# Attention in its fixed order: reciprocal roots of the RMS norm on VectorE instead of ScalarE

## The chip, the cores and the metric

The kernel runs on one core of a Trainium2 chip. The metric is the device time of one execution in microseconds (us), as the median of several runs. Five engines take part: TensorE (PE: matmuls and transposes; PEld: its weight loads), VectorE (DVE), ScalarE (ACT), GpSimd (POOL) and SyncE (SP, which issues most DMAs). Each engine runs its own instructions in order and waits for the others by semaphores.

## The reference, cut to what matters

Three layers follow each other: an attention with RMS-normalised queries and keys, a dense layer pair, and a mixture of experts. The change lies in the norm of the attention.

```python
# q, k, v: (4, 12, 448, 64); g_q, g_k: (64,)
def rmsnorm(x, g):
    rms = np.sqrt(np.mean(x * x, axis=-1, keepdims=True) + 1e-06)
    return x / rms * g
q_n, k_n = (rmsnorm(q, g_q), rmsnorm(k, g_k))
scores = (1 / np.sqrt(64)) * np.matmul(q_n, k_n.transpose(0, 1, 3, 2))
scores = scores - np.max(scores, axis=-1, keepdims=True)
attn = np.exp(scores)
attn = attn / (np.sum(attn, axis=-1, keepdims=True) + 1e-09)
x = np.matmul(attn, v)                     # then (1792, 768)
h = x @ w_in; x = np.maximum(0.01 * h, h) @ w_out
# then: each row of x goes to the expert of its largest gate logit (8 experts)
```

## The kernel before

The attention works on pairs of heads: 4 batches with 6 pairs each make 24 pairs. For one pair, q and k lie in SBUF as 112 partitions by 4 rows of 64 numbers, for two heads; that is one tile `qk` of 112x1024. The steps of a pair are:

- `square`: ACT squares `qk` into `sq`, DVE sums each 64 numbers into `ms` (112x16 for a pair).
- `roots`: from `ms` the factors `y` = 1/sqrt(mean square + 1e-6). Mostly two pairs are taken together (112x32), in four of the 14 calls one pair (112x16). ACT computes Ln (`ln`), then Exp with scale -0.5 (a first `y`), its square (`a`) and -0.5 times the mean square (`hm`); DVE makes one Newton step of them with two instructions (lines 219 and 220).
- `norm`: POOL multiplies q or k by `y` (tile `qn`, line 238), 112x512 each; for the very first pair k is multiplied on DVE.
- `turn_q`, `turn_k`: PE transposes, ACT and DVE split the result into a high and a low part (`qh`, `ql`, `kh`, `kl`). The product g_q times g_k (`gg`) goes into the key side.
- `top`: PE multiplies queries by keys into the PSUM tile `tp`, of which there is one, and DVE takes the row maxima (`md`, line 275), four chunks per pair. `row` transposes the maxima into `mx`.
- `probs`: PE makes scores in the PSUM tile `sc`, of which there is one too, and ACT takes the Exp of them (`p`, or `pr` for the first of the four chunks; line 298).
- `values`, `sums`, `back`, `spread`, `scale`, `store`: PE multiplies by v (`av`, line 307), POOL adds the four `p` into `pr` (line 311), and the row sums divide the result.

A unit here is the work between one `pr` and the next: the scores and values of one pair, the row maxima of the next, and preparation of later ones. The first three units run by `begin`, the others by `steady`. Their order on PE, DVE, ACT and POOL is written out by hand (`tc.manual_schedule`). Two calls of `roots` come ahead of unit 0, two in unit 0, one each in units 2 and 3; then every second unit (5, 7, 9 and so on to 19) holds one, between the second and the third row maximum. From unit 8 on the units between them hold, at the same place, `work`: a decode of half a weight tile for the dense layers, five DVE instructions (lines 579 to 584), an ACT and a POOL instruction (line 586).

```python
            if begun and odd and three:
                self.norm(three, (1,))
            if begun and odd and self.group:
                self.roots(self.group)
                self.norm(four, (1,))
            self.work(i)
```

`three` and `four` are the pairs three and four ahead. After the attention the dense layers follow (`FirstMoe`, lines 614 to 669), then the routing and the experts; their order is set by a scheduler.

Of the kernel before, what the change touches and what calls it, by code (L numbers as in the profile page):

```python
# [9 lines left out]
F32 = mybir.dt.float32  # L10
F32R = mybir.dt.float32r
I32 = mybir.dt.int32
U32 = mybir.dt.uint32
AF = mybir.ActivationFunctionType
ALU = mybir.AluOpType
# [5 lines left out]
def attention_moe_moe2(  # L21
# [15 lines left out]
    nc = tc.nc  # L37
    P = 128
    B, H, S, DH = q.shape
# [6 lines left out]
    CP = 112  # L46
# [49 lines left out]
    nc.gpsimd.iota(pcol_i, pattern=[[0, 1]], base=0, channel_multiplier=1)  # L96
    pcol = cst.tile([P, 1], F32, name="pcol")
    nc.vector.tensor_copy(pcol, pcol_i)
    gg = cst.tile([P, 1], F32, name="gg")
    gk = cst.tile([P, 1], F32, name="gk")  # L100
    WG = 32
# [3 lines left out]
    def load_constants():  # L105
        for half in range(2):
            nc.scalar.dma_start(gg[half * DH:(half + 1) * DH, :], g_q.rearrange("(d o) -> d o", o=1))
            nc.scalar.dma_start(gk[half * DH:(half + 1) * DH, :], g_k.rearrange("(d o) -> d o", o=1))
        nc.vector.tensor_tensor(gg, gg, gk, ALU.mult)

    def load_gates():
        nc.sync.dma_start(wg[:, :, :NE], w_gate.rearrange("(c p) e -> p c e", p=P))
# [40 lines left out]
    class Attention:  # L153


        def __init__(self, pool, early, ps, pst):
            self.pool, self.early, self.ps, self.pst = pool, early, ps, pst
            self.PR, self.MX = [], []
            self.first = self.work = None
            self.after = []  # L160
            self.mask = pool.tile([P, CP], F32R, name="mask", bufs=1)
            self.eps = pool.tile([CP, 1], F32, name="eps", bufs=1)
            nc.vector.memset(self.eps, 1e-6)
            self.eps2 = pool.tile([CP, 1], F32, name="eps2", bufs=1)
            nc.vector.memset(self.eps2, -0.5e-6)
            nc.scalar.activation(self.mask, mrow.to_broadcast([P, CP]), AF.Copy)
            for i in range(2):
                pr = pool.tile([P, 2, S], F32, name=f"pr{i}", bufs=1)
                nc.vector.memset(pr, 1e-9)
                self.PR.append(pr)  # L170
            for i in range(2):
                md = pool.tile([CP, NC, P], F32, name=f"md{i}", bufs=1)
                nc.vector.memset(md, 0.0)
                self.MX.append(md)
# [13 lines left out]
        def square(self, st):  # L188

            n = 4 * NC  # L190
            flat = st["qk"].rearrange("p t h (c d) -> p (t h c) d", d=DH)
            sq = self.early.tile([CP, n, DH], F32, name="sq", bufs=2)
            for h in (slice(0, n // 2), slice(n // 2, n)) if st is self.first else (slice(0, n),):
                nc.scalar.activation(sq[:, h], flat[:, h], AF.Square)
                nc.vector.tensor_reduce(st["ms"][:, h], sq[:, h], AX.X, ALU.add)

        def together(self, sts):
# [7 lines left out]
        def roots(self, sts):  # L205

            ms = sts[0]["all"]
            n = 4 * NC
            w, full = n * len(sts), n * 2
            ln, hm, a, y0, y1 = (  # L210
                self.pool.tile([CP, full], F32, name=name, bufs=bufs)[:, :w]
                for name, bufs in (("ln", 1), ("hm", 1), ("a", 1), ("y0", 1), ("y", 3)))
            for i, st in enumerate(sts):
                st["yf"] = y1[:, i * n:(i + 1) * n]
            nc.scalar.activation(ln, ms, AF.Ln, scale=1.0 / DH, bias=self.eps)
            nc.scalar.activation(y0, ln, AF.Exp, scale=-0.5)
            nc.scalar.activation(a, y0, AF.Square)
            nc.scalar.activation(hm, ms, AF.Identity, scale=-0.5 / DH, bias=self.eps2)
            nc.vector.tensor_tensor(a, a, hm, ALU.mult)
            nc.vector.scalar_tensor_tensor(y1, a, 1.5, y0, ALU.add, ALU.mult)  # L220

        def tr(self):
            return self.ps.tile([P, S], F32, name="tr", bufs=TRB)
# [572 lines left out]
    att.first = att.load(0, 0)  # L796
    att.load_v(att.first)
    load_constants()
    wts = Weights()
    moe = FirstMoe(wts)  # L800
# [28 lines left out]
    y = my.tile([P, B, KD, S], F32, name="ysum")  # L829
# [280 lines left out]
```

## Time and profile before

| | |
|---|---|
| median of 3 runs | 1290.72 us (1290.34 to 1291.54) |
| profiled execution | 1289.88 us, of which its span is 1288.2 us |
| PE busy | 1179.9 us (92%) |
| DVE busy | 743.8 us (58%) |
| ACT busy | 544.9 us (42%) |
| POOL busy | 529.3 us (41%) |
| first `pr` | 24.87 us from the start |
| start of unit 21, the last but two | 339.24 us |

The times of a trace are counted from the start of its span. The busy shares are means over stages with different limits: the attention lies in about the first 400 us, the dense layers and the experts in the rest. An idle time in brackets stands before the instruction that ended it, with the engine that released it.

### The profile page before, as it was taken

The numbers are of one execution on the slowest core, as the hardware profiler recorded it, in microseconds if no ns is written. First come the engines' busy times: TensorE is split into PE (matmuls) and PEld (weight loads), VectorE is DVE, ScalarE is ACT, GpSimd is POOL, SyncE is SP. The second block draws the span as 40 slices with busy tenths as digits, with TensorE's granted clock in tenths as the row PEclk, the third lists the DMA queues.
The fourth block names the chain that finished last, engine by engine and source line by source line (L and its number), as shares of the span: only waits on it lengthen the run. The fifth ranks groups of instructions, "written<-read, shape, count | busy, mean of one in ns | idle before, by whom it ended". The sixth has DMA issues, their size and how long they took to land.

```text
span 1288.2 us, 19076 instructions
## 1 busy us (share of the span) xinstructions
PE 1179.9 (92%) x6988; PEld 943.5 (73%) x6988; DVE 743.8 (58%) x1166; ACT 544.9 (42%) x875; POOL 529.3 (41%) x365
## 2 busy tenths in 40 slices
PE   4779998998999988999999999999799999999997
PEld 2445554554556877888888888988678988898986
DVE  5555666665652788475857584235766149414556
ACT  5676667665533542222222222122435148324444
POOL 1555665665633554243434343120224126412334
PEclk9898989888989999999999999999979999999999
DMA  5211122101010222021212120052375229612456
GB/s 142 58 37 50 51 64 75 56 27 28 28 44 25 75 74 74 21 66 37 62 38 68 33 72 13 1 208 51 86 267 188 76 86 361 232 46 80 179 215 216
DMA packets 68082, 116.29 MB, mean 90 GB/s; under 512 B 6780, under 2 KB 45948, under 8 KB 67968
## 3 DMA queue, kind: packets, MB, share of 16 engines
q1 hardware_dynamic: 64528, 103.87, 25.4%
q0 software_dynamic: 3120, 11.02, 2.5%
q8 instruction: 57, 0.93, 0.3%
q14 instruction: 57, 0.47, 0.1%
q10 hardware_dynamic: 320, 0.00, 0.0%
HBM read 106.61 MB, written 12.58 MB: 93 GB/s over the span
## 4 chain that ended last, share of the span: by engine, by line
PE 65%; DVE 14%; ACT 7%; issue 6%; POOL 5%; DMA 2%; ACTq 0%; DVEq 0%; POOLq 0%; SPq 0%
PE sc L296 6%; PE av L307 6%; PE mp L644 4%; PE mo L625 4%; PE mo L626 4%; PE mo L627 4%; PE mp L645 4%; PE mp L646 4%; PE ph L988 3%; PE ph L986 3%; PE ph L987 3%; PE py L1004 3%; PE py L1002 3%; PE py L1003 3%; DVE top L581 2%
## 5 line engine op out<-in xcount | busy, mean ns | idle before, releaser
L311 POOL TENSOR_TENSOR pr<-pr,p 112x896 f32<-112x896 f32 x72 | 152.5, 2118 | 58.1 <-ACT p L298 35.5
L652 DVE TENSOR_TENSOR ysum<-mp,ysum 128x448 f32<-128x448 f32 x168 | 103.8, 621 | 113.0 <-PE mp L646 112.2
L644 PE MATMUL mp<-gh,w1h 128*128 128x448 f32 x384 | 145.6, 380 | 20.1 <-DVE ysum L652 16.4
L625 PE MATMUL mo<-xTh,w0h 128*128 128x448 f32 x384 | 142.2, 370 | 7.0 <-DVE g L632 3.4
L645 PE MATMUL mp<-gl,w1h 128*128 128x448 f32 x384 | 142.4, 371 | 0.0
L626 PE MATMUL mo<-xTl,w0h 128*128 128x448 f32 x384 | 142.0, 370 | 0.2 <-DVE xTl L63 0.2
L627 PE MATMUL mo<-xTh,w0l 128*128 128x448 f32 x384 | 141.2, 368 | 0.0
L646 PE MATMUL mp<-gh,w1l 128*128 128x448 f32 x384 | 140.8, 370 | 0.0
L63 POOL TENSOR_TENSOR gl<-g,gh 128x448 fp32r<-128x448 f32 x64 | 76.9, 1201 | 140.1 <-ACT gh L633 113.3
L586 POOL TENSOR_TENSOR raw<-raw,top 128x384 f32<-128x384 f32 x64 | 64.8, 1013 | 139.7 <-DVE raw L584 114.9
L275 DVE TENSOR_REDUCE md<-tp 112x2 f32<-112x896 f32 x96 | 104.5, 1089 | 23.6 <-PE tp L273 23.0
L1002 PE MATMUL py<-w2h,hT 128*128 128x384 f32 x288 | 99.7, 346 | 0.0
L644 PEld LDWEIGHTS mp<-gh,w1h 128*128 128x128 f32 x384 | 72.8, 190 | 35.3 <-DVE ysum L652 13.8
L1004 PE MATMUL py<-w2l,hT 128*128 128x384 f32 x288 | 96.8, 336 | 0.0
L1003 PE MATMUL py<-w2h,hL 128*128 128x384 f32 x288 | 96.5, 335 | 0.0
L988 PE MATMUL ph<-w1l,xgh 128*128 128x512 f32 x216 | 86.5, 400 | 4.2 <-DVE w1l L63 4.2
L986 PE MATMUL ph<-w1h,xgh 128*128 128x512 f32 x216 | 86.8, 402 | 0.0
L63 DVE TENSOR_TENSOR hL<-pt,hT 128x512 fp32r<-128x512 f32 x36 | 24.8, 689 | 106.2 <-ACTq L1012 59.4
L578 ACT ACTIVATE mag<-wd 128x384 f32<-128x384 f32 x64 | 35.4, 553 | 118.9 <-DVE top L581 62.3
L987 PE MATMUL ph<-w1h,xgl 128*128 128x512 f32 x216 | 85.6, 396 | 0.0
L625 PEld LDWEIGHTS mo<-xTh,w0h 128*128 128x128 f32 x384 | 72.4, 189 | 16.0 <-DVE g L632 3.7
L298 ACT ACTIVATE p<-sc 112x896 f32<-112x896 f32 x72 | 65.8, 913 | 42.0 <-PE sc L296 37.7
(200 smaller groups left out, 2583.0 us busy)
## 6 DMA issues: line engine op xcount, KB each, us to landing
r<-in_moe_w_dram SPq DMA_DIRECT2D x27, 1024.0 KB, 5.2
r<-in_moe_w_dram SPq DMA_DIRECT2D x36, 768.0 KB, 7.3
wd<-in_moe_w_in_dram SPq DMA_DIRECT2D x32, 384.0 KB, 3.3
wd<-in_moe_w_out_dram SPq DMA_DIRECT2D x32, 384.0 KB, 3.1
qk<-in_q_dram SPq DMA_DIRECT2D x24, 224.0 KB, 3.0
qk<-in_k_dram SPq DMA_DIRECT2D x24, 224.0 KB, 3.2
vv<-in_v_dram SPq DMA_DIRECT2D x24, 224.0 KB, 2.7
x2d<-xn SPq DMA_DIRECT2D x24, 224.0 KB, 2.9
```

The costliest lines, as they stand in the source:

```text
L311: nc.gpsimd.tensor_tensor(st["pr"][:CP], st["pr"][:CP], p, ALU.add)
L625: nc.tensor.matmul(ph, wh_[:, c], xh, start=(c == 0), stop=False)
L626: nc.tensor.matmul(ph, wh_[:, c], xl, start=False, stop=False)
L627: nc.tensor.matmul(ph, wl_[:, c], xh, start=False, stop=(c == KD - 1))
L644: nc.tensor.matmul(py, hi[:, sl], gh, start=(j == 0), stop=False)
L645: nc.tensor.matmul(py, hi[:, sl], gl, start=False, stop=False)
L646: nc.tensor.matmul(py, lo[:, sl], gh, start=False, stop=(j == GF - 1))
L986: nc.tensor.matmul(ph[n], xh[:, c], w1h[:, c, s_], start=(c == 0), stop=False)
L988: nc.tensor.matmul(ph[n], xh[:, c], w1l[:, c, s_], start=False, stop=(c == K1 - 1))
L1002: nc.tensor.matmul(py[n], hT[:, c], w2h[:, c, s_], start=(c == 0), stop=False)
L1003: nc.tensor.matmul(py[n], hL[:, c], w2h[:, c, s_], start=False, stop=False)
L1004: nc.tensor.matmul(py[n], hT[:, c], w2l[:, c, s_], start=False, stop=(c == K2 - 1))
```

## The change

The four ACT instructions of `roots` go, with their tables, and DVE does it all with nine small instructions: add 1e-6 to the sum, take the bits of the result as an integer times -0.5 plus a constant (a first estimate), then a cubic step of four instructions and a Newton step of three. The steps leave out constant factors; their product, `ROOT` squared for a query and a key, is divided out once in `gg`. The squares are scaled by 1/8 on ACT, so that their sum is the mean. Two constant tiles and their memsets go.

```diff
+    LAST = -21.33333396911621
+    ROOT = (LAST + 64 / 9) * 8 / 3
...
-        nc.vector.tensor_tensor(gg, gg, gk, ALU.mult)
+        nc.vector.scalar_tensor_tensor(gg, gg, ROOT ** -2, gk, ALU.mult, ALU.mult)
...
-            self.eps = pool.tile([CP, 1], F32, name="eps", bufs=1)
-            nc.vector.memset(self.eps, 1e-6)
-            self.eps2 = pool.tile([CP, 1], F32, name="eps2", bufs=1)
-            nc.vector.memset(self.eps2, -0.5e-6)
...
-                nc.scalar.activation(sq[:, h], flat[:, h], AF.Square)
+                nc.scalar.activation(sq[:, h], flat[:, h], AF.Square, scale=DH ** -0.5)
...
-            nc.scalar.activation(ln, ms, AF.Ln, scale=1.0 / DH, bias=self.eps)
-            nc.scalar.activation(y0, ln, AF.Exp, scale=-0.5)
-            nc.scalar.activation(a, y0, AF.Square)
-            nc.scalar.activation(hm, ms, AF.Identity, scale=-0.5 / DH, bias=self.eps2)
-            nc.vector.tensor_tensor(a, a, hm, ALU.mult)
-            nc.vector.scalar_tensor_tensor(y1, a, 1.5, y0, ALU.add, ALU.mult)
+            nc.vector.tensor_scalar(ms, ms, 1e-6, None, ALU.add)
+            nc.vector.tensor_scalar(
+                y.bitcast(I32), ms.bitcast(I32), -0.5, float(0x5F3759DF), ALU.mult, ALU.add)
+            nc.vector.tensor_tensor(a, y, y, ALU.mult)
+            nc.vector.tensor_tensor(a, a, ms, ALU.mult)
+            nc.vector.scalar_tensor_tensor(e, a, -10 / 3, a, ALU.add, ALU.mult)
+            nc.vector.scalar_tensor_tensor(y, e, 5.0, y, ALU.add, ALU.mult)
+            nc.vector.tensor_tensor(a, y, y, ALU.mult)
+            nc.vector.tensor_tensor(a, a, ms, ALU.mult)
+            nc.vector.scalar_tensor_tensor(y, a, LAST, y, ALU.add, ALU.mult)
```

On ACT, a steady unit with a root stood like this before, from the `pr` that starts the unit to the second `p` (`sp` holds row sums):

```order
L298 ACTIVATE pr_139<-sc 112x896
L254 ACTIVATE qh<-tr 128x448
L215 ACT_TABLE_LOAD
L215 ACTIVATE ln<-ms,eps 112x32
L216 ACT_TABLE_LOAD
L216 ACTIVATE y_1322<-ln 112x32
L217 ACTIVATE a<-y_1322 112x32
L218 ACTIVATE hm<-ms,eps_134 112x32
L298 ACTIVATE p<-sc 112x896
L323 COPY sp<-tr 128x224
```

The same stretch of ACT now (line numbers are two higher from `norm` on):

```order
L300 ACTIVATE pr_135<-sc 112x896
L256 ACTIVATE qh<-tr 128x448
L300 ACTIVATE p<-sc 112x896
L325 COPY sp<-tr 128x224
L300 ACTIVATE p<-sc 112x896
```

The six rows of lines 215 to 218 are gone between `qh` and `p`, and nothing has come in their place. Of 29 table loads one is left, ahead of the first ACT instruction.

On DVE, a steady unit with a root, from the low part of the keys to the reciprocal of the row sums (`r`), before:

```order
L266 SCALAR_TENSOR_TENSOR kl<-tr,gg,kh 128x448
L275 TENSOR_REDUCE md_141<-tp 112x2
L219 TENSOR_TENSOR a<-a,hm 112x32
L220 SCALAR_TENSOR_TENSOR y<-a,y_1619 112x32
L275 TENSOR_REDUCE md_141<-tp 112x2
L63 TENSOR_TENSOR ql<-tr,qh 128x448
L275 TENSOR_REDUCE md_141<-tp 112x2
L333 RECIPROCAL r<-av 112x8
```

The root's place on DVE now, from the row maximum ahead of it to `ql`:

```order
L277 TENSOR_REDUCE md_137<-tp 112x2
L213 TENSOR_SCALAR ms<-ms 112x32
L214 TENSOR_SCALAR y<-ms 112x32
L216 TENSOR_TENSOR a<-y 112x32
L217 TENSOR_TENSOR a<-a,ms 112x32
L218 SCALAR_TENSOR_TENSOR e<-a 112x32
L219 SCALAR_TENSOR_TENSOR y<-e,y 112x32
L220 TENSOR_TENSOR a<-y 112x32
L221 TENSOR_TENSOR a<-a,ms 112x32
L222 SCALAR_TENSOR_TENSOR y<-a,y 112x32
L277 TENSOR_REDUCE md_137<-tp 112x2
L63 TENSOR_TENSOR ql<-tr,qh 128x448
```

Nine rows stand where two stood; the root keeps its place among the row maxima. POOL's and SP's rows are the same in both kernels, in the same order. On PE two matmul groups of the dense layers (six instructions) stand eleven rows later than before; the rest is the same.

At the end of unit 0, the fourth root of the kernel stood on DVE before between the sums of squares and the halves of the next pair:

```order
L275 TENSOR_REDUCE md_143<-tp 112x2
L195 TENSOR_REDUCE ms<-sq 112x16
L219 TENSOR_TENSOR a<-a,hm 112x32
L220 SCALAR_TENSOR_TENSOR y<-a,y_375 112x32
L266 SCALAR_TENSOR_TENSOR kl<-tr,gg,kh 128x448
L63 TENSOR_TENSOR ql<-tr,qh 128x448
L275 TENSOR_REDUCE md_141<-tp 112x2 x2
```

And now:

```order
L193 TENSOR_REDUCE ms<-sq 112x16
L213 TENSOR_SCALAR ms<-ms 112x32
L214 TENSOR_SCALAR y<-ms 112x32
...
L222 SCALAR_TENSOR_TENSOR y<-a,y 112x32
L268 SCALAR_TENSOR_TENSOR kl<-tr,gg,kh 128x448
L63 TENSOR_TENSOR ql<-tr,qh 128x448
L277 TENSOR_REDUCE md_137<-tp 112x2 x2
```

Here too nine rows stand where two stood, ahead of `kl`, `ql` and the row maxima of unit 1.

## Rows read from the trace of the kernel before

**Rows 1.** The page's head: the span.

```profile
span 1288.2 us, 19076 instructions
```

**Rows 2.** The chain that ended last, 106 to 340 us, shares by engine and line.

```profile
by line: PE sc L296 25.5%; PE av L307 23.7%; PE tr L340 8.3%; PE tr L246 6.3%; PE tp L273 5.8%; ACT L215 4.4%; ACT L216 4.4%; PE av L330 3.9%; PE tr L280 3.6%; ACT p L298 2.8%; ACT qh L254 2.1%; PE tr L319 1.6%; DMA wd<-in_moe_w_out_dram 1.
```

**Rows 3.** Lines 215, 216, 219: ns min/median/max, first and last start; DVE's wait, times.

```profile
L215 ACT ACT_TABLE_LOAD  x14: 1283/1283/1283, 6.2 to 312.4; - x14
L215 ACT ACTIVATE ln<-ms,eps x14: 307/322/322, 8.8 to 313.7; 112x32 f32<-112x32 f32 x10, 112x16 f32<-112x16 f32 x4
...
L216 ACT ACT_TABLE_LOAD  x14: 1283/1283/1283, 9.1 to 314.0; - x14
...
L219 DVE TENSOR_TENSOR a<-a,hm x14: 166/192/1405, 11.1 to 316.0; 112x32 f32<-112x32 f32 x10, 112x16 f32<-112x16 f32 x4
...
  ACT hm L218: 49.8, 13
```

**Rows 4.** Windows of units: from:to, us; busy of PE, PEld, DVE, ACT, POOL; clock.

```profile
106.04:123.18 17.14, 14.70 (x106) 8.77 (x104) 8.38 (x13) 10.89 (x18) 9.26 (x7) 0.80 0.15 41
123.18:134.94 11.76, 11.76 (x106) 6.76 (x104) 7.95 (x11) 7.55 (x11) 7.30 (x5) 1.00 0.20 59
134.94:150.67 15.73, 13.29 (x106) 7.71 (x104) 8.35 (x13) 10.89 (x17) 9.29 (x7) 0.89 0.15 45
...
162.72:179.94 17.22, 14.78 (x106) 8.65 (x104) 8.34 (x13) 10.88 (x18) 9.78 (x7) 0.80 0.21 64
...
191.98:206.25 14.27, 11.83 (x106) 6.73 (x104) 8.25 (x13) 10.89 (x17) 9.39 (x7) 1.00 0.26 76
...
218.31:235.58 17.27, 14.83 (x106) 8.81 (x104) 8.38 (x13) 10.89 (x18) 9.58 (x7) 0.80 0.21 64
235.58:247.62 12.04, 12.03 (x106) 6.76 (x104) 10.20 (x16) 7.98 (x12) 7.91 (x6) 1.00 0.19 59
247.62:263.38 15.76, 13.32 (x106) 7.78 (x104) 8.35 (x13) 10.89 (x17) 9.59 (x7) 0.89 0.13 41
...
275.44:292.67 17.23, 14.79 (x106) 8.68 (x104) 8.35 (x13) 10.88 (x18) 9.77 (x7) 0.80 0.12 36
...
310.24:327.46 17.22, 14.84 (x106) 8.83 (x104) 7.13 (x12) 9.89 (x16) 9.24 (x7) 0.80 0.05 14
```

**Rows 5.** Timeline of unit 13, around its root: start us, us, engine, what.

```profile
220.50 1.28 ACT L215 ACT_TABLE_LOAD   x1
...
224.16 0.19 DVE L219 TENSOR_TENSOR a<-a,hm 112x32 f32<-112x32 f32 x1 [4.45 <-ACT hm L218]
224.39 0.19 DVE L220 SCALAR_TENSOR_TENSOR y<-a,y 112x32 f32<-112x32 f32 x1
...
224.98 0.65 PE L296 MATMUL sc<-qh,kh 64*112 64x448 f32 x2 [2.44 <-ACT p L298]
```

**Rows 6.** Timeline of unit 14, around its decode.

```profile
236.90 0.35 DVE L579 TENSOR_SCALAR top<-wd 128x384 int32<-128x384 int32 x1
...
239.68 1.09 DVE L275 TENSOR_REDUCE md<-tp 112x2 f32<-112x896 f32 x1
...
240.82 0.17 PEld L273 LDWEIGHTS tp<-kh,qh 64*112 64x112 f32 x2 [0.40 <-DVE md L275]
```

**Rows 7.** Timeline of unit 0, around the fourth root.

```profile
40.97 2.08 POOL L311 TENSOR_TENSOR pr<-pr,p 112x896 f32<-112x896 f32 x1
...
41.70 1.41 DVE L219 TENSOR_TENSOR a<-a,hm 112x32 f32<-112x32 f32 x1 [2.40 <-ACT hm L218]
...
42.15 1.01 PE L246 MATMUL tr<-ident,qn 112*128 112x112 f32 x4 [3.22 <-ACT mx L282]
```

**Rows 8.** Timeline around the second root, and of unit 2.

```profile
21.46 1.09 DVE L275 TENSOR_REDUCE md<-tp 112x2 f32<-112x896 f32 x1 [0.81 <-PE tp L273]
...
22.93 2.04 POOL L238 TENSOR_TENSOR qn<-qk,y 112x512 f32<-112x512 f32 x2 [9.85 <-DVE y L220]
...
68.93 0.19 DVE L219 TENSOR_TENSOR a<-a,hm 112x32 f32<-112x32 f32 x1 [3.72 <-ACT hm L218]
```

More of the change, by code (lines that the diff above doesn't have):

```diff
@@ L209, in roots @@
             w, full = n * len(sts), n * 2
-            ln, hm, a, y0, y1 = (
+            y, a, e = (
                 self.pool.tile([CP, full], F32, name=name, bufs=bufs)[:, :w]
-                for name, bufs in (("ln", 1), ("hm", 1), ("a", 1), ("y0", 1), ("y", 3)))
+                for name, bufs in (("y", 3), ("a", 1), ("e", 1)))
             for i, st in enumerate(sts):
-                st["yf"] = y1[:, i * n:(i + 1) * n]
-            nc.scalar.activation(ln, ms, AF.Ln, scale=1.0 / DH, bias=self.eps)
-            nc.scalar.activation(y0, ln, AF.Exp, scale=-0.5)
-            nc.scalar.activation(a, y0, AF.Square)
-            nc.scalar.activation(hm, ms, AF.Identity, scale=-0.5 / DH, bias=self.eps2)
-            nc.vector.tensor_tensor(a, a, hm, ALU.mult)
-            nc.vector.scalar_tensor_tensor(y1, a, 1.5, y0, ALU.add, ALU.mult)
+                st["yf"] = y[:, i * n:(i + 1) * n]
+            nc.vector.tensor_scalar(ms, ms, 1e-6, None, ALU.add)
[8 more added lines that the diff above has]
+            nc.vector.scalar_tensor_tensor(y, a, LAST, y, ALU.add, ALU.mult)
         def tr(self):
```

## The prediction

> **What bounds the kernel now.** I read the chain of waits first, for the stretch where the roots are computed. From 106 to 340 us PE's lines hold most of the chain, but ScalarE's lines 215 and 216 hold 4.4% each [rows 2]: 8.8% of 234 us, some 20 us, in which everything waited for ScalarE to change its table and take a logarithm and a first root. That is not what an average shows: ScalarE is busy only 42% of the span.
>
> Then the instructions of those lines. Each of the 14 roots loads a table twice, 1.283 us each time, and VectorE idles 49.8 us in 13 waits for the last of the four ScalarE instructions [rows 3], 3.83 us each.
>
> Third, one such wait in order of time [rows 5]. The table load begins at 220.50; VectorE's Newton step starts at 224.16 after 4.45 us of idling; PE gets its score tile back at 224.98 after 2.44 us of idling, because the Exp that empties the single score tile stands behind the root on ScalarE. So two chains cross the root: PE by way of that Exp, and VectorE's row maxima.
>
> Last, the units as windows [rows 4]. A unit with neither root nor decode takes 11.76 us and PE is busy in all of it; one with a decode 12.04. The eight units with a root take 17.14, 15.73, 17.22, 14.27, 17.27, 15.76, 17.23 and 17.22 us, together 131.84. Their PE clock column tells two costs apart. The unit of 14.27 us ran at full clock (1.00): its excess of 2.51 us over 11.76 is the stall of 2.44 us. The others show 0.80 or 0.89, so for part of the unit PE ran at 1.2 instead of 2.4 GHz, and PE's busy time grew from 11.83 to as much as 14.84 us. Each of these spells follows the stall, and the units without a stall have none.
>
> **The change, part by part.**
>
> *The eight steady roots.* All six rows of ScalarE go. What comes is nine small VectorE instructions, each needing the one before. The old pair of dependent ones started at 224.16 and 224.39 [rows 5], so 0.23 us apart, and I take 9 x 0.23 = 2.07 us for the new chain; the pair has the width of the new ones, and the operands of seven of them. Do they make PE wait in their turn? The decode answers it: at the same place in the unit VectorE is held from 236.90 to 239.68, 2.78 us, and PE then waits 0.40 us for the row maximum behind it [rows 6]. A block of 2.07 us is 0.71 us shorter, so PE should wait for nothing and the unit should become one without root: 11.76 us. Bounds: 11.76, as PE is then full, and 12.04, that of a unit with the longer block. The gain is 131.84 - 8 x 11.76 = 37.8 us, at the least 131.84 - 8 x 12.04 = 35.5. This contains the clock: 8 x 2.51 = 20.1 us of stall and 17.7 us of slow spells, which I expect to go with the stall that comes before each of them.
>
> POOL must not get in the way here. An old Newton step took 1.41 us instead of 0.19 when POOL was adding: it began at 41.70 and ended at 43.11, POOL's add ended at 43.05 [rows 7]. So VectorE's instructions on two SBUF tiles are held until POOL's running instruction ends. In a steady unit POOL's next product needs this very root and stands ahead of the adds, so POOL is idle meanwhile. The Trainium skill, in "SBUF — State Buffer", section "Who interferes with whom", says that a VectorE instruction with two SBUF inputs and a GpSimd instruction that reads SBUF exclude each other for the whole instruction. The trace agrees with its 1.41 us; the rule speaks against nine such instructions wherever POOL has work queued, and by it each of them could there wait for one add.
>
> *The roots ahead of the steady phase.* Here each goes by its own place, and bounds are wide. In general a root gives VectorE back its wait, 3.83 us on average [rows 3], and takes seven more instructions, 7 x 0.23 = 1.61: at best 2.2 us. Nothing is excluded down to zero where something else is late.
> - First root: from the logarithm's start at 8.8 to the Newton step at 11.1 and 0.4 us beyond, 2.7 us [rows 3]; now 2.1. Gain 0.6.
> - Second: the old ScalarE part was hidden behind the row maxima. The last of these ends at 22.55 and POOL takes the result at 22.93, 0.38 us later [rows 8]; now nine instructions stand behind that maximum. Loss 2.07 + 0.1 - 0.38, some 1.8 us.
> - Third: a wait of both chains, gain between 0 and 2.2; I take 1.2, as the later start takes half a microsecond and more of it.
> - Fourth: PE waited 3.22 us for ScalarE [rows 7], and that goes. But the adds are then queued on POOL and do not need this root, so the first new instruction waits for one add and lets the next add in ahead of the second instruction. VectorE then ends as late as before, and PE gains until it wants the row maxima behind it. Between 0 and 3.2; I take 1.0, nearer the blocked end, because of the 1.41 us.
> - Unit 2: VectorE's wait of 3.72 us [rows 8] less 1.61: 2.1. Unit 3: the same at best; I take 1.5.
>
> Sum 0.6 - 1.8 + 1.2 + 1.0 + 2.1 + 1.5 = 4.6 us; bounds from about -1 (only the second root's loss and half a microsecond of gain) to 9, and up to 3 us more for each slow spell that ends early there.
>
> *Costed at nothing.* The scale of the squares and the factor in `gg` change operands of instructions that are there anyway. The two memsets lie ahead of the first DMA's landing, with VectorE idle later; uncovered they would cost a tenth each. ScalarE's freed time beyond the waits (28 loads of 1.283 us and 56 small instructions) is worth nothing, since PE bounds the units. The six PE instructions that stand later in the dense layers I put at nothing, PE being busy before and behind them; a microsecond to either side if the order matters. SP's order is the same, and each load keeps its distance in units, which become 12 us instead of up to 17; they are 3 us transfers.
>
> **The sum.** 37.8 + 4.6 = 42.4 us off the profiled execution. That took 1289.88 us, 1.7 more than its span [rows 1], and lies 0.84 below the median of 1290.72. So 1289.88 - 42.4 = 1247.5; I say 1247.5 us, about 3.3% faster. What a measurement can tell from no change is 0.2%, 2.6 us.
>
> **The rivals.**
>
> *The fourth root is not blocked* (POOL lets the nine through, or they come between the adds). PE then keeps the 3.2 us instead of 1.0, and the slow spell of units 0 and 1 may shrink by up to 3: 1242. Against it the 1.41 us. Chance 0.14. With the forecast's 0.62 this makes the likeliest range 1240 to 1254.
>
> *Only the stalls go, and the slow spells stay*, because they come from the units' load and not from the idling. Then the eight units give 20.1 us and not 37.8: 1289.88 - 20.1 - 4.6 = 1265. For it: the unit with the same stall at full clock shows that stall and spell are not tied one to one. Against it: none of the units without a stall has a spell. Chance 0.11.
>
> *POOL takes the port in the steady units.* If one add of 2.08 us falls into each root, VectorE's block is 4.15 us, 1.37 longer than the decode's, and PE waits 0.40 + 1.37 = 1.8 us per unit: 8 x 1.8 = 14 us less gain, 1262, and more if the clock falls again. It needs POOL to be late by more than a microsecond when a unit begins. Chance 0.08.
>
> *Slower than before.* The same port, but with all three adds of a unit let in between the nine: a block of 2.07 + 3 x 2.08 = 8.3 us, 5.5 over the decode's, so PE waits 5.9 us and the slow spell comes behind, up to 3 more: 8.9 instead of the present mean of 37.8 / 8 = 4.7, and 8 x 4.2 = 33 us are lost: about 1320. It decides from the second add on, where PE's wait passes 2.51 us. Against it POOL's order: the product that needs the root comes first. Chance 0.03.
>
> *No difference*, if PE waited as long for something that lies right behind ScalarE in every unit: 0.02; the units without a root speak against it.
>
> **The numbers.** 1247.5 us, range 1240 to 1264: it holds the forecast, the first rival and the lower end of the port's, and leaves out the slow spells that stay, the slower case and no difference, under 2 in 10. Faster 0.95, same 0.02, slower 0.03.
>
> **What would show it.** In the changed kernel: one table load; nine instructions of some 0.19 us at 0.23 us spacing; units with a root at 11.8 to 12.0 us with PE busy throughout and the clock column at 1.00; the attention's last units some 42 us earlier and the dense layers and experts as long as before. In unit 0 an instruction of the fourth root that lasts over a microsecond. Wrong would be: steady roots whose instructions last as long as POOL's adds; clock columns of 0.8 in units without a stall; or a later stage that grows by what the attention has lost.

## The result, and the profile after

The changed kernel takes 1245.75 us (median of 4 runs, 1244.74 to 1247.01) against 1290.53 of the kernel before (4 runs, 1290.26 to 1291.54): ratio 0.9652 [0.9635, 0.9669], 3.5% faster. The prediction was 1247.5, 1.75 us too high. The profiled execution took 1244.74 us.

The head of the page of the changed kernel: ScalarE is 47.3 us less busy than before, VectorE 17.9 us more, PE 18.7 us less although its instructions are nearly the same.

```profile
span 1242.7 us, 19106 instructions
...
PE 1161.2 (93%) x6988; PEld 931.5 (75%) x6988; DVE 761.7 (61%) x1262; ACT 497.6 (40%) x791; POOL 529.5 (43%) x365
```

PE's shorter busy time is the clock: the same columns at full speed take less. The windows of units show where (columns as in [rows 4]). The first four rows are units 0 to 3, then a steady unit with a root and unit 18.

```profile
23.65:40.53 16.88, 13.85 (x74) 7.84 (x74) 11.79 (x20) 9.30 (x13) 8.48 (x7) 1.00 0.18 55
40.53:59.02 18.49, 15.13 (x106) 8.71 (x104) 11.76 (x20) 7.57 (x12) 11.63 (x8) 0.82 0.22 62
59.02:72.24 13.22, 12.00 (x106) 6.76 (x104) 9.63 (x20) 7.55 (x12) 7.08 (x6) 1.00 0.19 54
72.24:86.34 14.10, 12.74 (x112) 7.25 (x110) 12.82 (x23) 9.85 (x14) 8.42 (x5) 1.00 0.18 50
...
169.32:181.08 11.76, 11.76 (x106) 6.73 (x104) 9.57 (x20) 7.55 (x12) 9.59 (x7) 1.00 0.32 93
...
252.58:271.19 18.61, 14.60 (x106) 8.03 (x104) 12.24 (x19) 7.60 (x13) 9.27 (x7) 0.82 0.13 34
```

Units 0 to 3 of the kernel before, for comparison:

```profile
24.87:44.96 20.09, 13.77 (x74) 8.11 (x74) 11.92 (x15) 16.13 (x24) 9.82 (x8) 0.90 0.16 47
44.96:61.10 16.14, 14.69 (x106) 7.72 (x104) 7.94 (x10) 7.45 (x11) 8.82 (x6) 0.81 0.27 72
61.10:78.02 16.92, 13.44 (x106) 7.38 (x104) 8.45 (x13) 11.00 (x17) 8.43 (x7) 0.90 0.22 63
78.02:94.27 16.25, 13.25 (x112) 7.21 (x110) 11.74 (x17) 13.19 (x21) 7.57 (x5) 1.00 0.07 21
```

The eight units with a root take 11.76 us, seven times, and once 11.78, all at clock 1.00: 94.10 us, where [rows 4] give 131.84. That is 37.74 us. The stretch ahead of unit 4 is 7.93 us shorter (86.34 against 94.27). Unit 18, which holds no root, is 1.04 us longer, and the other units 0.2 together. So the last `pr` comes 44.40 us earlier (336.36 against 380.76), and what follows it, dense layers and experts, takes 906.34 us against 907.44.

The chain that ended last, 90 to 300 us, by line; ScalarE's 4.4% and 4.4% of [rows 2] are gone:

```profile
by line: PE sc L298 26.4%; PE av L309 26.3%; PE tr L342 7.7%; PE tr L248 7.5%; PE tp L275 6.5%; PE tr L282 4.3%; PE av L332 3.7%; DVE md L277 2.9%; PE tr L321 2.7%; DVE raw L586 2.6%; ACT qh L256 1.8%; DVE top L583 1.6%; DMA wd<-in_moe_w_ou
```

A steady root in order of time (start us, us, engine, what), to be read beside [rows 5]:

```profile
169.81 1.05 POOL L240 TENSOR_TENSOR qn<-qk,y 112x512 f32<-112x512 f32 x1
...
170.64 0.26 DVE L213 TENSOR_SCALAR ms<-ms 112x32 f32<-112x32 f32 x1
...
172.51 0.19 DVE L222 SCALAR_TENSOR_TENSOR y<-a,y 112x32 f32<-112x32 f32 x1
172.61 1.09 DVE L277 TENSOR_REDUCE md<-tp 112x2 f32<-112x896 f32 x1
172.78 1.04 POOL L240 TENSOR_TENSOR qn<-qk,y 112x512 f32<-112x512 f32 x1 [1.92 <-DVE y L222]
...
173.46 0.46 PE L298 MATMUL sc<-qh,kh 64*112 64x448 f32 x2
```

From 170.64 to 172.61 the nine take up VectorE for 1.97 us. POOL's product ahead of the root ends at 170.86, 0.22 us into the first of the nine, which lasts 0.26 us (0.17 where POOL is idle, in the kernel with the chain twice); from then on POOL idles 1.92 us until the root is there, so the other eight meet nothing of POOL's. PE takes the score tile back at 173.46 without an idle time in brackets.

The fourth root at the end of unit 0, beside [rows 7]:

```profile
37.63 4.27 POOL L313 TENSOR_TENSOR pr<-pr,p 112x896 f32<-112x896 f32 x2
...
39.05 0.71 DVE L213 TENSOR_SCALAR ms<-ms 112x32 f32<-112x32 f32 x1
...
39.87 2.07 DVE L214 TENSOR_SCALAR y<-ms 112x32 int32<-112x32 int32 x1
...
42.23 0.36 PE L298 MATMUL sc<-mx,mask 64*112 64x448 f32 x2
...
43.44 0.68 DVE L268 SCALAR_TENSOR_TENSOR kl<-tr,gg,kh 128x448 fp32r<-128x448 f32 x1
...
44.56 1.08 DVE L277 TENSOR_REDUCE md<-tp 112x2 f32<-112x896 f32 x1
...
45.70 0.45 PE L275 MATMUL tp<-kh,qh 64*112 64x448 f32 x2 [3.11 <-DVE md L277]
...
48.13 0.58 PE L298 MATMUL sc<-ql,kh 64*112 64x448 f32 x2
```

POOL makes two adds from 37.63 to 41.90. The first new instruction ends at 39.76, with the first add (half of 4.27 us after 37.63); the second ends at 41.94, with the second add. PE then idles 3.11 us for the row maximum behind the chain, and a pair of its matmuls that took 0.36 us ahead of that wait (42.23) takes 0.58 behind it (48.13): the slow spell of unit 1.

### The profile page after: what moved, and what is told of

It reads as the page before. It is cut to its first block, busy times and chain, and to the rows that moved or that the text cites. A ratio compares the mean times of both kernels' runs of the same rounds, so it can differ in the third digit from the quotient of the medians.

```text
span 1242.7 us, 19106 instructions
## 1 busy us (share of the span) xinstructions
PE 1161.2 (93%) x6988; PEld 931.5 (75%) x6988; DVE 761.7 (61%) x1262; ACT 497.6 (40%) x791; POOL 529.5 (43%) x365
## 4 chain that ended last, share of the span: by engine, by line
PE 65%; DVE 16%; issue 7%; POOL 5%; ACT 3%; DMA 3%; ACTq 0%; DVEq 0%; POOLq 0%; SPq 0%
PE sc L298 6%; PE av L309 6%; PE mp L646 4%; PE mo L627 4%; PE mo L628 4%; PE mo L629 4%; PE mp L647 4%; PE mp L648 4%; PE ph L990 4%; PE ph L988 3%; PE ph L989 3%; DVE top L583 3%; PE py L1006 3%; PE py L1004 3%; PE py L1005 3%
## 5 line engine op out<-in xcount | busy, mean ns | idle before, releaser
L63 POOL TENSOR_TENSOR w1l<-r,w1h 128x1024 fp32r<-128x1024 f32 x17 | 42.9, 2529 | 93.0 <-ACT w1h L952 75.1
```

What stands on the lines that cost most here:

```text
L63: engine.tensor_tensor(dst, src, hi.bitcast(F32), ALU.subtract)
```

## The experiments

The twelve kernels ran in three groups, each group on one chip with the kernel before: 1289.86 us for the first four, 1289.35 for the next four, 1288.79 for the last. Theory: two table loads per root cost a stall of PE and, behind it, a slow spell; VectorE's nine instructions fit into its slack; in the first units POOL holds them. Rivals: the spells come from the units' load; the gain lies in another part of the change; POOL or the length of the chain doesn't matter.

**The two halves of the change.** The first kernel uses the new chain in the eight steady roots only, the second in the first six only (the condition without its `not`); the other roots keep ScalarE's four instructions, with constants that fit the new `gg`.

```diff
+            if not getattr(self, 'late', False):
+                nc.scalar.activation(ln, ms, AF.Ln, bias=self.eps)
+                nc.scalar.activation(y0, ln, AF.Exp, scale=-0.5)
...
+                return
...
+                self.late = True
                 self.roots(self.group)
```

> The new chain in the eight steady roots only; the first six roots keep the old one on ScalarE. Theory (the steady units lose 37.8 us, the first units the rest): 1289.9 - 37.8 = 1252, units with a root at 11.76 us. Rival (the two parts depend on each other, or the later stages took part of the gain): more than 2 us off that value.

> The new chain in the first six roots only; the eight steady ones keep the old one on ScalarE. Theory: the first six give what the traces show ahead of unit 4 (its start moved from 94.27 to 86.34), 7.9 us, so 1282, and the steady units with a root stay at 14 to 17 us. Rival (the prediction's 4.6 us): 1285.

Measured: 1252.83 us, 0.9714 [0.9694, 0.9734], and 1284.07 us, 0.9954 [0.9936, 0.9971]. The steady half gives 37.0 us, its units 11.78 to 11.80 us; the first half gives 5.8, between the 7.9 of the traces and the forecast's 4.6, and its interval (3.7 to 8.3) holds both. Its trace again has unit 4 begin at 86.33 us; but this execution (1289.18) is the slowest of the five, and its steady units with a root, the same as before, take 134.35 us instead of 131.84, by longer slow spells. Together 42.8, and the whole change gave 44.8 (42.7 in its repetition below): the halves add up.

**Work in PE's wait.** The kernel before, with small matmuls of constants into spare columns of a PSUM bank, at the place where PE waits for the Exp behind the root; 36 of them, then 9.

```diff
+            if begun and odd and self.group:
+                for _ in range(FILL):
+                    nc.tensor.matmul(prev["av"][:, S + 8:BANK], ident, ones_mat[:, :BANK - S - 8], start=True, stop=True)
```

> The kernel before, with 36 small matmuls on PE in the place where it waits for the Exp in each steady unit with a root; their results go nowhere. Theory (the slow spells follow the idling of PE): the stall stays, the spells go, units with a root take 14.3 to 14.8 us, and the total falls by 12 to 18 us to 1272 to 1278 although work is added. Rival (the spells come from the units' load): no change or slower, with the clock column still at 0.80 to 0.89.

> The kernel before with 9 small matmuls on PE in the wait instead of 36: in the longer version each of the 72 PE instructions took 0.115 us, together 8.25 us, three times the wait. 9 should take 2.07 us, less than the wait of 2.44. Theory (the slow spells follow the idling): the stall stays and the spells go, the eight units with a root take 14.2 to 14.5 us at a clock column of 1.00, total 1270 to 1274. Rival (the spells come from the units' load): units at 15.7 to 17.3 us again, total 1288 to 1291.

With 36 matmuls 1319.91 us, 1.0229 [1.0206, 1.0252]. The filler was sized wrongly: two PE instructions for each matmul and 8.25 us in all, so that the units grew to 19.95 us.

```profile
110.08 8.25 PE L498 MATMUL av<-ones_mat,ident 128*128 128x56 f32 x72
```

Their clock was 1.00 in every root unit, which already speaks for the theory, but the time can't show it. With 9 matmuls it can: 1269.57 us, 0.9854 [0.9838, 0.987]. One of its eight units, by windows:

```profile
105.58:119.87 14.29, 14.00 (x124) 8.82 (x122) 8.25 (x13) 10.88 (x18) 9.01 (x7) 1.00 0.17 49
```

All eight last 14.22 to 14.30 us at clock 1.00, 114.21 together. Against 131.84 that is 17.6 us less, just the 17.7 us that the prediction put down to slow spells, and the kernel is 19.2 us faster for *added* work. The stall is still there as time; only PE's idling is gone. So the spells follow the idling, and the rival that ties them to the units' load falls.

**The old order without the table loads.** The kernel before, with Ln and Exp replaced by a function that needs no table; its root is then a Newton step from a straight line, not the reference's.

```diff
-            nc.scalar.activation(ln, ms, AF.Ln, scale=1.0 / DH, bias=self.eps)
-            nc.scalar.activation(y0, ln, AF.Exp, scale=-0.5)
+            nc.scalar.activation(ln, ms, AF.Identity, scale=1.0 / DH, bias=self.eps)
+            nc.scalar.activation(y0, ln, AF.Identity, scale=-0.5, bias=self.one5)
```

> The kernel before with its order and its four ScalarE instructions, but Identity in place of Ln and Exp, so that no table is loaded; the result is then a Newton step from a straight line and not the exact root. Theory (the table loads make nearly all of the wait): ScalarE's part takes 1.1 us, the Exp behind it is late by half a microsecond at most, units with a root take 11.8 to 12.3 us, total 1246 to 1252. Rival (the way through ScalarE and back is what costs): units of 13 us or more, total above 1256.

Measured: 1241.43 us, 0.9623 [0.9598, 0.9649], below what was expected and no slower than the changed kernel (the intervals overlap). Steady root units last 11.77 to 11.79 us at clock 1.00, though the four ScalarE instructions still stand ahead of the Exp and VectorE still waits for them:

```profile
145.07 0.31 ACT L217 ACTIVATE ln<-ms,eps 112x32 f32<-112x32 f32 x1
...
146.12 0.90 ACT L300 ACTIVATE p<-sc 112x896 f32<-112x896 f32 x1
146.24 0.19 DVE L221 TENSOR_TENSOR a<-a,hm 112x32 f32<-112x32 f32 x1 [1.85 <-ACT hm L220]
```

From 145.07 to 146.12 they take 1.05 us, which the units can hide. So taking the table loads away is enough for the whole gain; that the arithmetic moved to VectorE adds nothing that shows. (The numbers that this kernel computes are others, but what follows the last `pr` takes 906.75 us, half a microsecond from the changed kernel's 906.34.)

**The chain twice.** In the eight steady roots the nine instructions run once more ahead of the real ones, into tiles that nobody reads.

```diff
-                self.roots(self.group)
+                self.roots(self.group, twice=True)
```

> The changed kernel with the nine VectorE instructions run twice in the eight steady roots, first into tiles that nobody reads. Theory: a block of 4.14 us, 1.36 longer than the decode's 2.78, which makes PE wait 0.40: PE waits 1.7 us, units with a root take 13.3 to 13.5 us, or up to 16 with slow spells behind the wait: total 1258 to 1262 without spells, up to 1282 with them. Rival (VectorE has room enough): less than 4 us more.

Measured: 1259.82 us, 0.9756 [0.9728, 0.9783]. Two of its windows:

```profile
97.69:110.81 13.12, 12.02 (x106) 6.72 (x104) 11.02 (x29) 7.56 (x12) 8.93 (x7) 1.00 0.17 53
...
147.78:162.44 14.66, 13.48 (x106) 7.82 (x104) 11.16 (x29) 7.55 (x12) 9.57 (x7) 0.88 0.24 76
```

In the first of them the chain ends and the row maximum begins at 102.86, 3.86 us after the chain's start at 99.00, and PE waits:

```profile
104.00 0.45 PE L288 MATMUL tp<-kh,qh 64*112 64x448 f32 x2 [1.10 <-DVE md L290]
```

PE idles 0.77 to 1.18 us in the eight units, not the 1.7 that was expected, and slow spells come back in four of them. The total lies in the range that was given for no spells, 1258 to 1262, by luck: a wait that is too short and spells that were left out offset each other. VectorE's slack for a root lies between the 1.97 us of one chain, at which PE doesn't wait, and these 3.86.

**POOL's queue filled.** Two additions of constants on POOL, ahead of the product that needs the root.

```diff
+                for _ in range(2):
+                    nc.gpsimd.tensor_tensor(
+                        junk, ones_mat[:CP].unsqueeze(1).to_broadcast([CP, 4, P]),
+                        ident[:CP].unsqueeze(1).to_broadcast([CP, 4, P]), ALU.add)
                 self.roots(self.group)
```

> The changed kernel with two more POOL instructions of about 1.05 us, from constant tiles into a tile that nobody reads, ahead of the product that needs the root in the eight steady units. Theory (an instruction of VectorE on two SBUF tiles is held until POOL's running one ends): two of the nine instructions last about 1 us, the block grows to some 4 us, PE waits 1.3 to 1.8 us, total 1256 to 1262 and more with slow spells. Rival (no holding): the nine stay at 0.19 us each, and the total within 3 us of the changed kernel, as POOL has room for it.

Measured: 1268.14 us, 0.9824 [0.9799, 0.9849]. A unit's root in order of time:

```profile
154.94 0.26 DVE L213 TENSOR_SCALAR ms<-ms 112x32 f32<-112x32 f32 x1
155.11 2.70 POOL L487 TENSOR_TENSOR junk<-ones_mat,ident 112x512 f32<-112x512 f32 x2
...
155.30 1.15 DVE L214 TENSOR_SCALAR y<-ms 112x32 int32<-112x32 int32 x1
...
156.49 0.19 DVE L216 TENSOR_TENSOR a<-y 112x32 f32<-112x32 f32 x1
156.71 1.15 DVE L217 TENSOR_TENSOR a<-a,ms 112x32 f32<-112x32 f32 x1
...
158.91 1.08 DVE L277 TENSOR_REDUCE md<-tp 112x2 f32<-112x896 f32 x1
...
160.05 0.46 PE L275 MATMUL tp<-kh,qh 64*112 64x448 f32 x2 [1.22 <-DVE md L277]
```

Each of POOL's two instructions holds one of the nine until it ends (the held ones end at 156.45 and 157.86; POOL's two run from 155.11 to 157.81), and between them one VectorE instruction passes. Held is not only an instruction with two operands from SBUF but also line 214, which has one. From the first of the nine to the row maximum it is 3.97 us instead of 1.97 (154.94 to 158.91), PE waits 1.22 us, a little under the 1.3 to 1.8 that were expected, and the units grow to 12.99 and 13.24 us at full clock and, in the six that draw a slow spell, to 14.70 to 14.82; with the spells the time passes the 1256 to 1262 of the holding alone. Being held by POOL is thus a real price, which the steady units of the changed kernel escape because POOL waits for the root there.

**The tables back.** The changed kernel with one Ln of constants on ScalarE in each steady root unit; nobody reads it.

```diff
+                nc.scalar.activation(junk, ones_mat[:CP, :8 * NC], AF.Ln)
                 self.roots(self.group)
```

> The changed kernel with one small Ln on ScalarE, of a constant tile into a tile that nobody reads, at the old place in the eight steady units: two table loads each come back, and VectorE waits for nothing of it. Theory (PE is held by the Exp behind the tables, and VectorE's own wait costs little more): ScalarE's part is 2.9 instead of 3.6 us, PE waits 1.8 us in each, and slow spells follow in most of the units: 8 times 1.8 to 4.8, total 1260 to 1284. Rival (VectorE's wait was what bound): within 4 us of the changed kernel.

Measured: 1273.05 us, 0.9863 [0.9838, 0.9887]. A unit in order of time, and two windows:

```profile
99.91 0.55 ACT L256 ACTIVATE qh<-tr 128x448 fp32r<-128x448 f32 x1 [0.71 <-PE tr L248]
...
100.47 1.28 ACT L486 ACT_TABLE_LOAD   x1
...
101.77 0.23 ACT L486 ACTIVATE junk<-ones_mat 112x32 f32<-112x32 f32 x1
...
102.01 1.28 ACT L300 ACT_TABLE_LOAD   x1
...
104.28 0.46 PE L298 MATMUL sc<-qh,kh 64*112 64x448 f32 x2 [1.79 <-ACT p L300]
```

```profile
98.28:114.86 16.58, 14.79 (x106) 8.69 (x104) 9.60 (x20) 10.24 (x14) 9.32 (x7) 0.79 0.14 43
...
126.64:140.27 13.63, 11.84 (x106) 6.78 (x104) 9.51 (x20) 10.25 (x14) 9.33 (x7) 1.00 0.18 51
```

The two loads alone bring back a stall of PE, and the eight units take 122.26 us instead of 94.10. Only ScalarE's part of the old root was put back, and three quarters of the loss in the steady units came with it (28.2 of 37.7 us).

**The fourth root moved.** The changed kernel; the fourth root leaves the end of unit 0 for unit 1, behind `kl`, `ql` and the first row maximum.

```diff
-                        [("square", 4), ("roots", 3, 5)]]
+                        [("square", 4)]]
-                todo = [[("norm", 3)], [("square", 5)], [("norm", 4)], []]
+                todo = [[("roots", 3, 5), ("norm", 3)], [("square", 5)], [("norm", 4)], []]
```

> The changed kernel with the fourth root moved from the end of unit 0 to unit 1, behind the halves kl and ql and the first row maximum, where POOL's adds are done. Theory (the fourth root is held by POOL's adds and keeps the row maxima waiting): no instruction of it over 0.3 us, unit 1 shorter by 3 us or more (PE waited 3.11 us there), total 1242 to 1244. Rival (unit 1 is bound by something behind it): total as the changed kernel, 1245 to 1247.

Measured: 1239.74 us, 0.9606 [0.9582, 0.963], better than expected. Unit 1, and its root:

```profile
40.10:53.53 13.43, 12.19 (x106) 6.73 (x104) 10.01 (x20) 7.46 (x11) 11.36 (x8) 1.00 0.29 85
```

```profile
41.31 0.51 DVE L213 TENSOR_SCALAR ms<-ms 112x32 f32<-112x32 f32 x1
...
41.92 0.18 DVE L214 TENSOR_SCALAR y<-ms 112x32 int32<-112x32 int32 x1
```

Unit 1 falls from 18.49 to 13.43 us: PE's busy time from 15.13 to 12.19 (the spell, 2.9 us) and its idle time from 3.36 to 1.24 (2.1 us). One instruction is still held a little, by the tail of an add that ends at 41.78. The changed kernel's 1245.75 us is from another chip; in the two traces unit 4 begins at 80.86 us instead of 86.34, which is 5.5 of the 6.0 us.

**More roots moved.** On top of that, the second root ahead of the last row maximum (second kernel here), and a square and the fifth root each a place earlier (third); then the changed kernel again, on the same chip.

```diff
-                self.roots(sts[1:2])
+                    if c == 2:
+                        self.roots(sts[1:2])
...
-                todo = [[("roots", 3, 5), ("norm", 3)], [("square", 5)], [("norm", 4)], []]
+                todo = [[("roots", 3, 5), ("norm", 3)], [("square", 5)], [("norm", 4)], [("square", 6)]]
...
-                todo = [[("square", 6)], [("roots", 5, 7), ("norm", 5)], [("norm", 6)], []]
+                todo = [[("roots", 5, 7), ("norm", 5)], [], [("norm", 6)], []]
```

> The fourth root later, as in the run before, and the second root moved ahead of the last row maximum of the first pair, where the sum it needs is ready. Theory (the second root keeps POOL and then PE waiting, 1.66 us on PE): unit 0 shorter by 0.5 to 1 us, pr of unit 0 later by about 1, total the same as with the fourth root alone or up to 1 us less, 1239 to 1240. Rival (the row maximum it delays costs more): 1 us slower or more.

> Both moves, and the square and the root of unit 2 each one step earlier, so that the root no longer stands ahead of the row maximum that the reciprocal waits for. Theory (PE waited 0.97 us for that reciprocal): unit 2 shorter by up to 1 us, total 1238 to 1240. Rival (the root is in the way of another row maximum there): no gain.

> The changed kernel once more, beside the moved ones on the same chip, to compare with them: 1245.8 with a point of spread, units as in its first profile; unit 18 between 17.6 and 18.7 us, where it differed between kernels that are alike there.

Measured: 1238.98 us, 0.9612 [0.9596, 0.9628]; 1238.25 us, 0.961 [0.9593, 0.9627]; the changed kernel again 1246.13 us, 0.967 [0.965, 0.9689]. The second and third moves can't be told from the first alone by their time: their intervals overlap that of the fourth root's move. Their traces show what was expected all the same: with the second root moved PE no longer waits behind the first `pr`, which comes 0.9 to 1.3 us later, and unit 0 takes 13.89 and 14.74 us instead of the 16.58 with the fourth root's move alone; with the third move unit 2 takes 12.16 us instead of 13.22:

```profile
53.17:65.33 12.16, 11.91 (x106) 6.77 (x104) 8.50 (x19) 6.61 (x10) 8.86 (x8) 1.00 0.35 96
```

What stands is that the moved versions beat the changed kernel on the same chip by 7.2 and 7.9 us. Units 0 and 1 of the changed kernel in its repetition:

```profile
24.18:40.17 15.99, 12.93 (x74) 7.28 (x74) 11.80 (x19) 9.29 (x12) 7.67 (x6) 1.00 0.22 58
40.17:60.87 20.70, 16.45 (x106) 9.10 (x104) 12.54 (x21) 7.56 (x11) 12.45 (x9) 0.75 0.21 55
```

## Why the prediction was right, step by step

- **The steady roots: right.** Forecast 37.8 us, measured 37.74. The block was 1.97 us instead of 2.07, and PE did not wait. POOL was idle for the reason given, and the experiment with a filled queue shows what it would have cost otherwise. The decode was the right row to judge the block by, but its price was misread: the 0.40 us in [rows 6] stand before PEld, the weight load. PE's own matmul there (240.83) has no idle time in brackets. It begins 0.39 us after the one ahead of it (240.44), where 0.20 is usual (174.17 to 174.37 in the changed kernel), so PE lost 0.19 us. Redone in this way, the three blocks in this place agree: the decode's 2.78 us cost 0.19, the double chain's 3.86 cost 1.26 (102.54 to 104.00), and the filled queue's 3.97 cost 1.38 (158.47 to 160.05), each the block less some 2.6 us. By this estimate, 2.6 us of slack on VectorE, the forecast for the nine stands as it was; the 1.7 and 1.8 us of waiting, expected for the double chain and for the rival of POOL, started from 0.40 and came out 0.2 us too long.
- **Stall and spell: right.** Filling the wait removed the 17.6 us of the spells and left the stall; taking the tables away removed both, and bringing the tables back, or a VectorE block that is too long, brought back both.
- **The roots ahead of the steady phase: a size was off.** The term of 4.6 us measured 7.93 in the profile, and 5.8 us by the medians of the kernel that has this half alone. It differs between executions: in the repetition of the changed kernel unit 2 begins at 60.87 us instead of 59.02, after a longer slow spell in unit 1, and the term is 6.1. By its parts: first `pr` and units 0 and 1 were forecast at 0.6 - 1.8 + 1.2 + 1.0 = 1.0 and gave 1.22 + 3.21 - 2.35 = 2.1. The last row maximum ahead of the second root begins 1.21 us earlier (20.25 against 21.46 of [rows 8]), twice what I gave the first root, though 0.36 of it isn't the root's: the sums of squares ahead of it begin that much earlier (7.09 against 7.45), behind a product that waits for a load. POOL takes the second root 1.82 us after the end of that maximum instead of 0.38, a loss of 1.4, not 1.8. Units 2 and 3 were forecast at 3.6 and gave 3.70 + 2.15 = 5.85. In unit 2 the idling shrank by 2.26 us, as the 2.1 said, but PE's busy time also fell, from 13.44 to 12.00 at clock 1.00: a slow spell ended there, which I had only in the bound.
- **The fourth root: right as a mechanism, its gain too large.** Its first instruction was held by one add and its second by the next, as forecast, and VectorE came to `kl` at 43.44, where it had come at 43.31 before. The rival that it wouldn't be blocked falls. That rival's price was too small: 2.2 us and up to 3, 1242 us, where the moved root gave 1239.7. PE's waits in units 0 and 1 tell the terms apart. For the third root PE waited 1.72 us before and doesn't now (forecast 1.2). The second root's wait, 0.20 us before, is 1.66 now. The fourth root gave PE next to nothing by itself: a wait of 3.11 us for the row maxima, and 4.00 in the repetition, in place of 3.22 for ScalarE, with a slow spell behind it, where I took a gain of 1.0; the 1.20 us that PE waited for the reciprocal later in unit 1 is gone too. Together units 0 and 1 gained 3.21 - 2.35 = 0.86 us, and in the repetition lost 0.5, where 0.4 was forecast (-1.8 + 1.2 + 1.0).
- **Costed at nothing: about right.** From the last `pr` to the end it is 1.1 us shorter, which is within the spread of that stretch (904.9 to 909.1 us over all traces here), so the displaced PE instructions of the dense layers cost nothing that shows. Unit 18 (no root, no part of the change) is 1.04 us longer, but lasted between 17.6 and 19.0 us in the experiments too, in kernels that are the same there; its cause stays open.
- **The sum.** 37.74 + 7.93 - 1.04 - 0.2 + 1.1 = 45.5 us of span; outside the span the profiled execution gained 0.4 less, so 45.1 against the forecast's 42.4. Of the 2.7 us, 3.3 come from the first units and 1.1 from the later stages, less the rest. The medians differ by 44.8.
- **The rivals.** Slow spells that stay (1265): refuted by the eight units at clock 1.00, and in their reason by the filled wait. POOL taking the port (1262): not here, but 1268 when forced. Slower, and no difference: no sign of either.

Rows for the waits named above, of the kernel before:

```profile
35.02 0.46 PE L296 MATMUL sc<-qh,kh 64*112 64x448 f32 x2 [1.72 <-ACT p L298]
...
240.83 0.46 PE L273 MATMUL tp<-kh,qh 64*112 64x448 f32 x2
```

And around the second root of the changed kernel, beside [rows 8]:

```profile
20.25 1.09 DVE L277 TENSOR_REDUCE md<-tp 112x2 f32<-112x896 f32 x1 [0.81 <-PE tp L275]
...
23.16 2.04 POOL L240 TENSOR_TENSOR qn<-qk,y 112x512 f32<-112x512 f32 x2 [11.31 <-DVE y L222]
...
25.26 1.75 PE L248 MATMUL tr<-ident,qn 112*128 112x112 f32 x8 [1.66 <-POOL qn L240]
```

Weighing the Trainium skill: in "SBUF — State Buffer", section "Who interferes with whom", it counts `tensor_scalar`, which reads a single tile, with those that can exclude GpSimd, where it runs in a two-port mode. The trace agrees that it can be held: lines 213 and 214 lasted 0.71 and 2.07 us, each until an add of POOL's ended; in which mode they ran no run here shows. I had argued from instructions on two SBUF tiles alone, by which these two would have passed; the forecast of them was right and its reason too narrow. The Trainium skill, in "ScalarE: Activation LUTs", section "What ACT_TABLE_LOAD costs", gives 1283 ns for the load and some 1380 ns more for a drain at every switch. The load agrees to the nanosecond [rows 3]; the drain doesn't show here: in the kernel with the tables back the Ln starts at 101.77, 0.02 us after its load ends, and the load itself at 100.47, 0.01 after the instruction ahead, so the measured price of a switch is 1.30 us.

## What to carry to other kernels

Price a stall of PE with what comes behind it: here 20.1 us of stall drew another 17.7 us of slow clock, and neither shows in the average busy shares of ScalarE and VectorE. Before moving a chain to VectorE, find a row in the same place that shows how long a block PE tolerates, and ask what POOL has queued at that moment: a chain of nine costs 1.97 us where POOL waits for its result, and 3.97 us where two of POOL's instructions stand ahead. In such a row, read PE's idle time and not that of its weight loads. Where the runs show POOL in the way, move the chain: the fourth root at another place of the order was worth some 6 us.

## What the runs showed of the hardware that was not expected

- The same stall draws a spell in one unit and none in the next: in the kernel with the tables back, units with the same two loads took 13.63 us at clock 1.00 (three of eight), 15.09 at 0.89 (one) and 16.52 to 16.60 at 0.79 (four). What decides between them stays open.
- A wait filled with matmuls of constants made the kernel before 1.5% faster: 17.6 of the 19.2 us are the slow spells of the eight units.
- With POOL's queue filled, each of POOL's two instructions held just one VectorE instruction. In six of the eight units one VectorE instruction passed between the two that were held (156.49 to 156.71 in that timeline); in the other two units, as in the fourth root, the very next one was held.
